# Seven block products for the second product of a feed-forward layer, in an fp32 kernel for one core

## The chip, the core and the metric

One NeuronCore of a Trainium2 chip runs the whole kernel. Its engines are TensorE (PE, matrix products; PEld is its weight load), VectorE (DVE), ScalarE (ACT), GpSimd (POOL) and SyncE (SP, which here only issues DMAs). Each engine works through its own list of instructions in order and waits at semaphores for the others. The metric is the device time of one execution, in microseconds (us).

## The reference, cut to what matters

```
x = attention(q, k, v)                       # retention, 4 x 576 tokens, 512 wide
h = x @ moe_w_in;  g = max(0.01*h, h);  y = g @ moe_w_out       # first layer
h = y @ moe2_w_in; g = h * cos(h);      out = g @ moe2_w_out    # second layer
```

There are 2304 tokens; both layers go from 512 to 2048 and back to 512, all in fp32. For accuracy the kernel splits each fp32 operand into a high part that TensorE takes exactly and the remainder, and adds three products (high by low, low by high, high by high). So each block product is made of three matmuls per 128 rows of depth.

## The kernel before, in words

**First part of the program.** Attention and the first layer run over five blocks of tokens (512, 512, 512, 384, 384), and the result y goes to DRAM. Beside this, the second layer's operands are prepared and stored in DRAM: `second_weights` (L1009) converts the weights of a pair of 128-wide slices of the hidden layer, `x_parts` (L902) makes the forms of y.

**Second layer, first product.** Tokens are taken in three blocks of 768 (two halves of 384), the hidden layer in eight pairs of slices. One block with one pair is a unit; there are 24 units. A unit is a 2 x 2 block product done with seven block products in place of eight (the scheme of Strassen and Winograd): sums and differences of the blocks of the weights (`wa`, `ws`) and of y (`xq`) are made beforehand, and partial results are shared between PSUM banks 4 to 7 by ScalarE copies (L1212). `i_mm` (L1106) is one such product: six matmuls of 128x128 by 128x384.

**Gate.** `gate` (L1130) makes g = h cos(h) of one 128x384 block at a time: copy or add out of PSUM, the integer number of turns (ScalarE), two steps that take the turns away (VectorE, L1150 and L1155), a sine and a square (ScalarE, L1162 and L1163), one product (VectorE, L1166), then the high part (ScalarE, L1173) and the remainder (VectorE, L1176).

**Second layer, second product.** `out_` (L1225) takes one token half, one of four output slices and one unit: two slices of the hidden layer, three matmuls each, six matmuls. Two units make a group that adds up in one PSUM bank (0 to 3); after each group VectorE adds the bank, times -2, to the sum in SBUF (L1258), or into the buffer that is stored. A group has 2 halves x 2 units x 4 slices = 16 such steps, and there are 12 groups.

**What sets the order.** `slots` is a list in program order: one second product behind about every first product, and what is left of each block at its end (`LATE`, `DRAIN`). Everything after the first block of tokens is then given as tasks to `Plan`, with an assumed duration, what it needs and a due time. `play` always takes, of the tasks that can begin first, the one that is due first, and so fixes the order of each engine's list, SP's too. Buffers are handed out in rings (`Ring`), and a ring's size decides when a load may start. `open_low` and `open_all` open the second layer's buffers when those of the first part are done with.

## Time and profile before

| | us |
|---|---|
| median of 3 runs | 855.56 (853.37 to 856.75) |
| the profiled execution | 853.42 |
| its span, first to last instruction | 851.3 |
| TensorE busy in the span | 829.3 (97%) |
| VectorE busy | 601.5 (71%) |
| ScalarE busy | 518.4 (61%) |

The span is the time between the first and the last instruction of the profiled execution; what lies around it is 2.1 us. Matrix instructions are pipelined, so the mean duration of one (334 ns) is longer than the distance between two; the distance is read from the chain of waits, which gives the length of a run of so many matmuls. The chain is followed back from the last instruction: at each step to whatever ended the wait, or to the instruction before on the same engine.

### The profile page before, as it was taken

How to read it: one execution, taken by the hardware profiler on the slowest of the kernel's cores; microseconds unless marked ns; L12 is line 12 of the kernel's file. 1: busy time of each engine (PE TensorE's matmuls, PEld its weight loads, DVE VectorE, ACT ScalarE, POOL GpSimd, SP SyncE). 2: the span in 40 equal slices, each digit the busy share in tenths (PEclk: the TensorE clock that was granted, in tenths of full speed). 3: DMA queues.
4: the chain of work that ended last, by engine and by line, in shares of the span. 5: the costliest groups of instructions: out<-in, count | busy, mean ns of one | idle time of the engine just before them, and what ended most of it. 6: DMA issues, size and time to landing. Idle time of an engine off the chain costs nothing.

```text
span 851.3 us, 16302 instructions
## 1 busy us (share of the span) xinstructions
PE 829.3 (97%) x6288; PEld 771.0 (91%) x6288; DVE 601.5 (71%) x1183; ACT 518.4 (61%) x1112; POOL 8.5 (1%) x9
## 2 busy tenths in 40 slices
PE   6699999999999999999999999999999999999998
PEld 6478888888888888999999999999999999999998
DVE  4799985776876757667511587889877876866762
ACT  4688864554655545555422688767678755677650
POOL 0000020000000000000000000000000000000000
PEclk7799999999999999999999999999999999999999
DMA  9925512656657866853790798798988697665312
GB/s 358 418 83 202 192 67 85 217 194 211 211 191 251 247 213 197 260 191 135 262 406 2 252 311 272 265 374 322 349 284 287 216 405 272 208 225 186 137 49 75
DMA packets 91949, 193.30 MB, mean 227 GB/s; under 512 B 7648, under 2 KB 55264, under 8 KB 81632
## 3 DMA queue, kind: packets, MB, share of 16 engines
q1 hardware_dynamic: 91728, 191.92, 64.2%
q8 instruction: 49, 0.80, 0.4%
q10 hardware_dynamic: 144, 0.35, 0.1%
q14 instruction: 28, 0.23, 0.1%
HBM read 143.22 MB, written 49.02 MB: 226 GB/s over the span
## 4 chain that ended last, share of the span: by engine, by line
PE 90%; DMA 4%; issue 3%; DVE 2%; ACT 1%; SPq 0%; POOLq 0%; DVEq 0%
PE psum L1239 23%; PE psum L519 22%; PE psum L505 21%; PE psum L1111 19%; DMA raw<-in_w 2%; PE psum L366 1%; PE psum L305 1%; PE psum L328 1%; PE psum L268 1%; DMA wa<-wa 1%; DMA ws<-ws 1%; DVE t L464 0%; DVE st L351 0%; DVE t L457 0%; DVE t L453 0%
## 5 line engine op out<-in xcount | busy, mean ns | idle before, releaser
L1239 PE MATMUL psum<-g,wo 128*128 128x384 f32 x1152 | 222.3, 334 | 0.0
L505 PE MATMUL psum<-x_sb,w 128*128 128x512 f32 (+1 forms) x960 | 214.2, 373 | 4.2 <-DVE x_sb L493 2.5
L519 PE MATMUL psum<-g,w 128*128 128x512 f32 (+1 forms) x960 | 212.0, 370 | 0.0
L505 PEld LDWEIGHTS psum<-x_sb,w 128*128 128x128 f32 x960 | 177.5, 190 | 29.7 <-DVE x_sb L493 2.7
L1239 PEld LDWEIGHTS psum<-g,wo 128*128 128x128 f32 x1152 | 201.7, 188 | 0.0
L519 PEld LDWEIGHTS psum<-g,w 128*128 128x128 f32 x960 | 174.3, 188 | 23.7
L1111 PE MATMUL psum<-x,ws 128*128 128x384 f32 x576 | 114.5, 335 | 1.3 <-ACT psum L1212 1.3
L1111 PEld LDWEIGHTS psum<-x,ws 128*128 128x128 f32 x576 | 100.9, 188 | 2.3 <-ACT psum L1212 1.9
L797 DVE TENSOR_TENSOR g<-graw,g 128x512 fp32r<-128x512 f32 (+1 forms) x64 | 39.9, 623 | 69.3 <-ACT g L794 69.0
L1111 PE MATMUL psum<-x,wa 128*128 128x384 f32 x432 | 86.1, 334 | 0.0
L1111 PEld LDWEIGHTS psum<-x,wa 128*128 128x128 f32 x432 | 75.9, 188 | 0.0
L1166 DVE SCALAR_TENSOR_TENSOR h<-r,h 128x384 f32<-128x384 f32 x96 | 52.9, 554 | 24.0 <-ACT r L1163 23.7
L794 ACT CAST g<-graw 128x512 fp32r<-128x512 f32 (+1 forms) x64 | 36.3, 568 | 48.8 <-PE psum L519 47.0
L790 ACT ACTIVATE graw<-psum 128x512 f32<-128x512 f32 (+1 forms) x64 | 34.7, 542 | 48.2 <-PE psum L505 47.5
L1162 ACT ACTIVATE r<-r 128x384 f32<-128x384 f32 x96 | 50.4, 525 | 21.2 <-DVE r L1155 20.7
L1150 DVE SCALAR_TENSOR_TENSOR r<-n,h 128x384 f32<-128x384 int32 x96 | 53.0, 552 | 11.9 <-ACT n L1147 11.5
L1176 DVE TENSOR_TENSOR g<-h,g 128x384 fp32r<-128x384 f32 x96 | 52.7, 553 | 10.9 <-ACT g L1173 10.3
L1147 ACT ACTIVATE n<-h 128x384 int32<-128x384 f32 x96 | 49.3, 519 | 8.4 <-DVE h L1139 8.0
L1155 DVE SCALAR_TENSOR_TENSOR r<-n,r 128x384 f32<-128x384 int32 x96 | 53.2, 554 | 1.6
L1173 ACT CAST g<-h 128x384 fp32r<-128x384 f32 x96 | 48.6, 509 | 7.6 <-DVE h L1166 7.3
L1163 ACT ACTIVATE r<-r 128x384 f32<-128x384 f32 x96 | 50.5, 526 | 2.0
L1258 DVE SCALAR_TENSOR_TENSOR acc<-psum,acc 128x384 f32<-128x384 f32 x48 | 26.7, 557 | 16.4 <-PE psum L1239 15.3
(81 smaller groups left out, 794.8 us busy)
## 6 DMA issues: line engine op xcount, KB each, us to landing
ws<-ws SPq DMA_DIRECT2D x24, 1024.0 KB, 7.1
wo<-wo SPq DMA_DIRECT2D x24, 1024.0 KB, 6.0
wa<-wa SPq DMA_DIRECT2D x24, 768.0 KB, 6.1
ch<-in_qkv SPq DMA_DIRECT2D x17, 1024.0 KB, 7.7
mraw<-in_w SPq DMA_DIRECT2D x64, 256.0 KB, 3.6
x<-xq SPq DMA_DIRECT2D x21, 768.0 KB, 9.6
raw<-in_w SPq DMA_DIRECT2D x15, 1024.0 KB, 9.1
xq<-m SPq DMA_DIRECT2D x84, 128.0 KB, 5.1
```

The costliest lines, as they stand in the source:

```text
L505: nc.tensor.matmul(hp, wt[:, i, cols], x_t[lj, k][:, j, :n], start=(k == 0 and a == 0), stop=(k == KK - 1 and a == 2),)
L519: nc.tensor.matmul(psum[:, BANK_O + m, :n], wt[:, i, cols], gt[:, j, :n], start=(f == 0 and a == 0), stop=(f == NF - 1 and a == 2),)
L1111: nc.tensor.matmul(bank[BANKS[m]], a[:, hl, i, j * P : (j + 1) * P], x[:, j, v, :], start=m in (1, 5) and j == 0 and n == 0, stop=j == 1 a ...
L1147: t = add("ACT", 515, lambda: nc.scalar.activation(n_ap(), hb.ap, AF.Copy, scale=INV_2PI), [t], due, 0, nb.old)
L1150: nc.vector.scalar_tensor_tensor(out=r_ap(), in0=n_ap(), scalar=-C1, in1=hb.ap, op0=ALU.mult, op1=ALU.add)
L1155: nc.vector.scalar_tensor_tensor(out=r_ap(), in0=n_ap(), scalar=-C2, in1=r_ap(), op0=ALU.mult, op1=ALU.add)
L1162: t = add("ACT", 515, lambda: nc.scalar.activation(r_ap(), r_ap(), AF.Sin, scale=0.5), [t], due)
L1163: t = add("ACT", 515, lambda: nc.scalar.activation(r_ap(), r_ap(), AF.Square), [t], due)
L1166: nc.vector.scalar_tensor_tensor(out=hb.ap, in0=r_ap(), scalar=0.5, in1=hb.ap, op0=ALU.subtract, op1=ALU.mult)
L1173: t = add("ACT", 515, lambda: nc.scalar.copy(gb.ap[:, 0], hb.ap), [t], due, 0, gb.old)
L1176: nc.vector.tensor_tensor(out=gb.ap[:, 1], in0=hb.ap, in1=gb.ap[:, 0].bitcast(F32), op=ALU.subtract)
L1239: nc.tensor.matmul(bank[m], wt[:, i, hl, m * P : (m + 1) * P], gt[:, v, :], start=h == 0 and z == 0 and x == 0, stop=h == 1 and z == 1 and ...
```

## The change

The first part of the program keeps its products. In the second layer:

- The second product is a 2 x 2 block product by seven products too. A group is again two units; its blocks are (hidden slice pair) by (token halves), and each product works on both units and one of two output slices `t`: 14 products of six matmuls per group. The order of the products is `OUT`; each `t` has two PSUM banks, `a` and `b`, and ScalarE copies `a` to `b` twice per group and `t` (`cp1`, `cp2`).
- Its weights are forms of w_out, `wp` (four) and `wq` (three) per pair of slices, made in `second_weights` with the factor -4 pi, in place of `wo`. Both rings hold two.
- The gate counts in turns: the forms of w_in carry the factor 1/(2 pi), so one step takes the turns away in place of two, and it works on two blocks (768 columns) at once. It also makes the sums that the seven products need (`tq`), and splits two blocks at a time.
- Weights are walked to and fro: the second block of tokens takes the pairs from the last to the first, so that the first two units of a block use the weights that lie there.
- TensorE's two kinds of products are two chains for the planner, no longer one. The forms of y for the second block of tokens are made in the first part of the program. The forms lie in DRAM and SBUF in pieces of 128 tokens, and a matmul of the first product reads its 384 columns as three pieces.

```diff
+OUT = (1, 6, 2, 7, 3, 5, 4)
+O_OF = {1: ("p", 0), 6: ("p", 1), 2: ("p", 2), 7: ("p", 3), 3: ("q", 0), 4: ("q", 1), 5: ("q", 2)}
-LATE, DRAIN = 12, 6
+LATE, LAST, DRAIN = 8, 10, 5
-N_G, N_WO, N_H = 16, 4, 6
+N_G, N_Z = 9, 2
...
-        todo = [x for g in range(n_unit // 2) for x in halves(g)]
+        todo = [("o", g, m, t) for g in range(n_unit // 2) for m in OUT for t in range(2)]
...
-                debt = min(debt + 8 / 7, 2.0) if ripe() else 0.0
+                debt = min(debt + 1, 2.0) if ripe() else 0.0
...
+            made, last = w_sums(*quarter, got, d[7], [(o2, 2), (o1, 3), (o1, 1), (o2, 0)], BACK)
+            last += [
+                parted(quarter[0], tb[0], [(o1, 0)], [made], d[7], BACK),
+                parted(lambda b=tb[1]: b.ap, tb[1], [(o1, 2), (o2, 1)], [made], d[7], BACK),
+            ]
...
+                if u >= NPAIR and u % NPAIR < 2:
+                    same = u - 1 - 2 * (u % NPAIR)
+                    w_buf[kind, u], w_task[kind, u] = w_buf[kind, same], w_task[kind, same]
...
-                        bank[BANKS[m]],
+                        bank[BANKS[m]].rearrange("p (q t) -> p q t", t=Q),
                         a[:, hl, i, j * P : (j + 1) * P],
-                        x[:, j, v, :],
+                        x[:, :, v, j, :],
...
-            t = dve(600, rest_a, [t], due, rb.old)
-            t = dve(560, rest_b, [t], due)
-            nb.users.append(t)
-            t = add("ACT", 515, lambda: nc.scalar.activation(r_ap(), r_ap(), AF.Sin, scale=0.5), [t], due)
-            t = add("ACT", 515, lambda: nc.scalar.activation(r_ap(), r_ap(), AF.Square), [t], due)
+            def turn():
                 nc.vector.scalar_tensor_tensor(
+                    out=rb.ap, in0=rb.ap.bitcast(I32), scalar=-1.0, in1=pair(), op0=ALU.mult, op1=ALU.add
+                )
+            t = dve(1040, turn, [t], due)
+            t = add("ACT", 885, lambda: nc.scalar.activation(rb.ap, rb.ap, AF.Sin, scale=PI), [t], due)
+            t = add("ACT", 885, lambda: nc.scalar.activation(rb.ap, rb.ap, AF.Square), [t], due)
...
+            t13 = dve(960, from_b, [*both, opened["all"]], due, tq.old)
+            t2 = dve(560, lambda: then(2, 2, 0), [t13], due)
+            two("z", z_ring, lambda: hb.ap[:, 3:4], 1, [t], hb)
+            t4 = dve(560, lambda: then(3, 3, 2), [t2], due)
+            two("u", g_ring, lambda: q(2, 4), 2, [t4], tq)
+            two("t", g_ring, lambda: q(0, 2), 2, [t13, t2], tq)
...
-            if h == 0:
+            if m == 1:
+                read_at[g, "cp1", t] = add(
+                    "ACT", 490, lambda: nc.scalar.copy(b, a), [got, b_free.get(t) or bank_free[2 + t][0]], due - SOON
+                )
                 return
...
+            if m == 2:
+                read_at[g, "cp2", t] = add(
+                    "ACT", 490, lambda: nc.scalar.copy(b, a), [read_at[g, 6, t], x], due - SOON
+                )
...
             (0, 0, at["H", 2, 4]), (0, 1, at["H", 2, 8]), (0, 2, at["H", 2, 12]),
+            (1, 0, at["H", 3, 4]), (1, 1, at["H", 3, 9]), (1, 2, at["H", 3, 14]),
```

How the lists move is shown at three places. First TensorE, where the first second products stand behind the third unit; before (L1111 is the first product, L1239 the second):

```order
L1111 MATMUL psum<-x_4506,wa_4510 128x384 x6
L1111 MATMUL psum<-x_4507,ws_4512 128x384 x6
L1239 MATMUL psum<-g_4876,wo_4514 128x384 x3
L1239 MATMUL psum<-g_4877,wo_4514 128x384 x3
L1111 MATMUL psum<-x_4508,ws_4512 128x384 x6
L1239 MATMUL psum<-g_4876,wo_4514 128x384 x3
L1239 MATMUL psum<-g_4877,wo_4514 128x384 x3
```

And now (L1143 is the first product, L1315 the second), four first products into the fourth unit:

```order
L1143 MATMUL psum<-x_4820,wa_4825 128x384 x6
L1315 MATMUL psum<-g_5109,wp_5104 128x384 x3
L1315 MATMUL psum<-g_5112,wp_5105 128x384 x3
L1315 MATMUL psum<-g_5109,wp_5104 128x384 x3
L1315 MATMUL psum<-g_5112,wp_5105 128x384 x3
L1143 MATMUL psum<-x_4821,ws_4827 128x384 x6
L1143 MATMUL psum<-x_4822,ws_4827 128x384 x6
L1143 MATMUL psum<-x_4823,wa_4825 128x384 x6
```

The first second product stood behind 19 first products and stands behind 25 now; a second product reads two units' weights (`wp_5104` and `wp_5105`) where it read one unit's.

Second, VectorE at the end of the program, where the last gate ends; before (L1176 is the remainder of g, L1258 the addition of a PSUM bank):

```order
L1166 SCALAR_TENSOR_TENSOR h_4864<-r_4871,h_4864 128x384
L1258 SCALAR_TENSOR_TENSOR acc_4891<-psum,acc_4891 128x384
L1176 TENSOR_TENSOR g_4890<-h_4864,g_4890 128x384
L1258 SCALAR_TENSOR_TENSOR acc_4891<-psum,acc_4891 128x384 x3
L1258 SCALAR_TENSOR_TENSOR out_4873<-psum,acc_4891 128x384
```

And now (L1352 adds a PSUM bank, L1232 and L1235 make the sums `tq`, L1214 is the remainder of a form):

```order
L1214 TENSOR_TENSOR z_5118<-h_4829,z_5118 128x384
L1352 TENSOR_TENSOR acc_5120<-psum,acc_5120 128x384
L1214 TENSOR_TENSOR z_5119<-h_5103,z_5119 128x384
L1214 TENSOR_TENSOR g_5114<-tq_5108,g_5114 128x2x384
L1232 TENSOR_TENSOR tq_5108<-h_5103 128x768
L1235 TENSOR_TENSOR tq_5108<-h_5103,tq_5108 128x384 x2
L1214 TENSOR_TENSOR g_5117<-tq_5108,g_5117 128x2x384
L1214 TENSOR_TENSOR g_5116<-tq_5108,g_5116 128x2x384
L1352 TENSOR_TENSOR acc_5120<-psum,acc_5120 128x384 x7
```

Behind the last gate's product stand a subtraction of two blocks, two more that hang on it, and three remainders, where one remainder stood; and the last addition of the group before the last (the first L1352 shown) now stands ahead of them.

Third, SP's list just ahead of the second layer's first loads; before (L880 stores a prepared form, L1091 loads weights, L1102 loads forms of y):

```order
L756 DMA y<-graw 128x384
L880 DMA wo_108<-mt 128x512
L880 DMA wo_108<-mraw 128x512
L880 DMA wo_108<-mt 128x512
L880 DMA wo_108<-mraw 128x512
L1091 DMA wa_4510<-wa_85 128x1536
L1091 DMA ws_4512<-ws_93 128x2048
```

And now (L886, L1123 and L1134 are the same three):

```order
L886 DMA xq_83<-mt 128x256 x3
L886 DMA xq_83<-more 128x256 x2
L886 DMA xq_83<-mt 128x256 x2
L886 DMA xq_83<-more 128x256 x6
L886 DMA xq_83<-mt 128x256
L886 DMA xq_83<-more 128x256
L1123 DMA wa_4824<-wa_85 128x1536
L1123 DMA ws_4826<-ws_93 128x2048
L1134 DMA x_4817<-xq_82 128x1536
```

The stores of the forms of y for the second block of tokens now stand ahead of the first load; before they stood among the second layer's loads.

## Rows read from the trace of the kernel before

**Rows 1.** The page, busy time of TensorE, its share of the span, instructions.
```profile
PE 829.3 (97%) x6288; PEld 771.0 (91%) x6288; DVE 601.5 (71%) x1183; ACT 518.4 (61%) x1112; POOL 8.5 (1%) x9
```

**Rows 2.** Span and mean granted TensorE clock of the core.
```profile
core 0: 851.3 us, clock 0.986
```

**Rows 3.** Stretches: length, PE, PEld, DVE, ACT, POOL busy, clock, DMA share, GB/s.
```profile
440.00:445.00 5.00, 5.00 (x31) 5.00 (x30) 0.56 (x1) 1.50 (x3) 0.00 (x0) 1.00 1.01 417
...
460.00:480.00 20.00, 20.00 (x117) 20.00 (x116) 5.59 (x11) 7.35 (x14) 0.00 (x0) 1.00 0.37 106
480.00:500.00 20.00, 18.75 (x106) 17.83 (x104) 15.62 (x31) 17.15 (x39) 0.00 (x0) 1.00 0.95 314
500.00:520.00 20.00, 19.92 (x115) 19.83 (x115) 16.36 (x34) 17.29 (x40) 0.00 (x0) 1.00 0.87 317
560.00:580.00 20.00, 20.00 (x117) 20.00 (x116) 16.46 (x33) 14.78 (x34) 0.00 (x0) 1.00 1.03 412
```

**Rows 4.** Groups of instructions by line, TensorE: shapes, count, busy us, mean ns, idle before.
```profile
L1239 PE MATMUL psum<-g,wo 128*128 128x384 f32 x1152 | 222.3, 334 | 0.0
...
L1111 PE MATMUL psum<-x,ws 128*128 128x384 f32 x576 | 114.5, 335 | 1.3 <-ACT psum L1212 1.3
...
L1111 PE MATMUL psum<-x,wa 128*128 128x384 f32 x432 | 86.1, 334 | 0.0
```

**Rows 5.** The chain that ended last, longest pieces: start us, us, what.
```profile
140.13 8.64 PE psum L505 x36
...
471.21 7.30 PE psum L1111 x42
...
487.34 6.70 DMA wa<-wa
...
819.75 28.10 PE psum L1239 x162
```

**Rows 6.** The chain's last piece.
```profile
847.87 0.56 DVE out L1258
```

**Rows 7.** Groups by line, VectorE.
```profile
L1155 DVE SCALAR_TENSOR_TENSOR r<-n,r 128x384 f32<-128x384 int32 x96 | 53.2, 554 | 1.6
...
L476 DVE TENSOR_TENSOR w<-t,w 128x1024 fp32r<-128x1024 f32 (+1 forms) x17 | 19.8, 1165 | 2.9 <-ACT w L473 2.9
...
L873 DVE TENSOR_TENSOR m<-m 128x512 fp32r<-128x512 f32 x24 | 16.3, 687 | 4.7 <-ACT m L869 4.0 <-DMA xq<-m 0.5
...
L890 DVE TENSOR_TENSOR m<-m 128x256 f32<-128x256 f32 x24 | 9.2, 420 | 1.4 <-DMA m<-y 1.3
```

**Rows 8.** Groups by line, ScalarE.
```profile
L1163 ACT ACTIVATE r<-r 128x384 f32<-128x384 f32 x96 | 50.5, 526 | 2.0
...
L1212 ACT COPY psum<-psum 128x384 f32<-128x384 f32 x48 | 22.4, 466 | 16.4 <-PE psum L1111 15.1
...
L446 ACT ACTIVATE raw<-raw 128x1024 int32<-128x1024 uint32 (+1 forms) x17 | 18.8, 1104 | 0.0
...
L473 ACT CAST w<-t 128x1024 fp32r<-128x1024 f32 (+1 forms) x17 | 17.1, 1004 | 2.8 <-DVE t L464 2.7
...
L869 ACT CAST m<-m 128x512 fp32r<-128x512 f32 x24 | 14.6, 617 | 5.1 <-DMA xq<-m 5.1
```

**Rows 9.** Instructions of VectorE in order of time: start us, us, what.
```profile
586.82 0.56 DVE L1139 TENSOR_TENSOR h<-psum,s 128x384 f32<-128x384 f32 x1
587.30 0.55 DVE L1166 SCALAR_TENSOR_TENSOR h<-r,h 128x384 f32<-128x384 f32 x1
```

**Rows 10.** DMA issues: line, count, KB each, median us from issue to landing.
```profile
ws<-ws SPq DMA_DIRECT2D x24, 1024.0 KB, 7.1
...
x<-xq SPq DMA_DIRECT2D x21, 768.0 KB, 9.6
```

**Rows 11.** SP's list in order of time: start us, us, what.
```profile
419.51 0.40 SPq L1091 DMA_DIRECT2D wa<-wa  x1
...
431.44 0.32 SPq L1091 DMA_DIRECT2D wo<-wo  x1
```

More of the change, by code (lines that the diff above doesn't have):

```diff
@@ L1150, in rest_a @@
+            half_done[u, m] = read
+            if m in (2, 3):
+                return read
+            first = m == 7
+            due = by["x" if first else "u"] - AHEAD
+            pair = lambda: hb.ap[:, 0:3:2] if first else hb.ap[:, 1:4:2]
+            rb = r_ring.next()
+            t = add(
+                "ACT", 885, lambda: nc.scalar.copy(rb.ap.bitcast(I32), pair()),
+                [read, half_done[u, 2 if first else 3]], due, 0, rb.old,
+            )
+            def turn():
                 nc.vector.scalar_tensor_tensor(
-                    out=r_ap(), in0=n_ap(), scalar=-C1, in1=hb.ap, op0=ALU.mult, op1=ALU.add
+                    out=rb.ap, in0=rb.ap.bitcast(I32), scalar=-1.0, in1=pair(), op0=ALU.mult, op1=ALU.add
@@ L1171, in gate @@
             rb.users.append(t)
[L1172 to L1182 removed]
+            half_done[u, first] = t
@@ new lines, in two, with lower @@
+            def two(kind, ring, src, n, needs, buf):
+                due = by[kind] - AHEAD / 4
+                gb = g_buf[u, kind] = ring.next()
+                def lower():
+                    nc.vector.tensor_tensor(
+                        out=gb.ap[:, :, 1], in0=src(), in1=gb.ap[:, :, 0].bitcast(F32), op=ALU.subtract
+                    )
+                h_ = add("ACT", 885 if n == 2 else 515, lambda: nc.scalar.copy(gb.ap[:, :, 0], src()),
+                         [*needs, opened["all"]], due, 0, gb.old)
+                t = dve(960 if n == 2 else 560, lower, [h_], due)
+                buf.users.append(t)
+                g_low_done[u, kind] = t
@@ new lines, in gate, with from_b, then @@
+            if first:
+                two("x", g_ring, pair, 2, [t], hb)
+                return read
+            tq = tq_ring.next()
+            both = [t, half_done[u, True]]
+            q = lambda i, j: tq.ap[:, i:j]
+            def from_b():
+                nc.vector.tensor_tensor(out=q(0, 2), in0=hb.ap[:, 1:3], in1=hb.ap[:, 0:2], op=ALU.subtract)
+            def then(i, b, a):
+                nc.vector.tensor_tensor(out=tq.ap[:, i], in0=hb.ap[:, b], in1=tq.ap[:, a], op=ALU.subtract)
@@ L1247, in out_ @@
[L1247 to L1259 removed]
+                            to,
@@ new lines, in mm @@
+                            wt[:, hl, i, t * P : (t + 1) * P],
+                            gt[:, fi, v, :],
+                            start=m in (1, 5) and h == 0 and x == 0,
+                            stop=h == 1 and x == 2,
+                            skip_group_check=True,
+                        )
+            got = last_pe["o"] = add("PE", 1042, mm, needs, due)
+            for u in us:
+                w_buf[kind, u].users.append(got)
+                g_buf[u, form].users.append(got)
@@ L1273, in out_ @@
-            bank_free[m] = [t]
+                x = add(
+                    "ACT", 490, lambda: nc.scalar.copy(kept(), to),
+                    [got, opened["all"], left.get((which, t))], due - SOON / 2,
+                )
+            else:
+                x = add("DVE", 560, lambda: nc.vector.tensor_tensor(out=kept(), in0=to, in1=kept(), op=ALU.add),
+                        [got], due - SOON / 2)
+            read_at[g, m, t] = x
+            if last and m in (2, 4):
+                leave(x, which, m == 4, 0)
@@ new lines, in out_, with more @@
+            if last and m == 5:
+                for w, half, other in ((1, 0, 3), (3, 1, 7)):
+                    def more(w=w):
+                        nc.vector.tensor_tensor(
+                            out=acc.ap[:, 2 * w + t], in0=acc.ap[:, 2 * w + t], in1=acc.ap[:, 8 + t], op=ALU.add
+                        )
+                    y = dve(560, more, [x, read_at[g, other, t]], due - SOON / 2)
+                    leave(y, w, half, 1)
+                    left[4, t] = y
+            if m == 2:
+                read_at[g, "cp2", t] = add(
+                    "ACT", 490, lambda: nc.scalar.copy(b, a), [read_at[g, 6, t], x], due - SOON
+                )
```

308 lines of the change are left out of this document (155 added, 153 removed).

## The prediction

> **What bounds the kernel now.** I read the page first. TensorE is busy for 97% of the span [rows 1] at a mean granted clock of 0.986 [rows 2], so the end is set by how much TensorE has to do, and the other engines matter only where they keep it waiting. The stretches show where that is. From 460 us on TensorE is busy for 20.00 us of 20 but for the beginning of the second layer, where 1.25 us are lost between 480 and 500 and 0.08 behind that, at a clock of 1.00 throughout [rows 3]. VectorE has some 16.4 us of work in 20 there. The chain agrees: its long pieces are TensorE's, it enters the second layer at 471.21 and leaves TensorE at 847.85, ahead of one last addition on VectorE [rows 5, 6]. Between these lie 376.6 us in which 1152 + 576 + 432 = 2160 matmuls of 384 columns run [rows 4].
>
> The price of one matmul is taken from the chain, not from its own duration: the last 162 take 28.10 us, 0.1735 us each; 42 at the stage's start take 7.30, the same [rows 5]. 2160 of them are 374.8 us, and with the 1.3 us of waits this is the stage to within half a microsecond. One block product (six matmuls) is 1.041 us.
>
> **What is removed.** A group has 14 products in place of 16, and there are 12 groups: 24 products or 144 matmuls fewer, 144 x 0.1735 = 25.0 us. All of them stand on the path, since TensorE has no gap in which they could hide. The page "TensorE: Matmul & The Clock Gate" of the Trainium skill (section Back-to-back issue gap) gives an isolated spacing of columns / 2.4 + 2.5 ns, which is 162.5 ns here, and for a stream of load and product 131 ns at 512 columns. By the first the gain would be 23.4 us, by the second under 19. The trace agrees with neither: 173.5 ns at 384 columns.
>
> **What is added on VectorE and ScalarE in the second layer.** VectorE's instructions take 420 ns at 256 columns, 687 at 512 and 1165 at 1024 [rows 7]; 768 lies half way between the last two, 0.93 us. Neighbours overlap: one of 0.56 us is followed 0.48 us later by the next [rows 9], so I count 0.48 for a narrow and 0.85 for a wide one. A unit now has two narrow additions out of PSUM, two wide steps that take the turns away, two wide products, one wide and two narrow sums, and three wide and one narrow remainder: 8 x 0.85 + 5 x 0.48 = 9.2 us. A group is two units and ten additions of a bank: 18.4 + 4.8 = 23.2 us in the 28 x 1.041 = 29.1 us that TensorE needs, 80%. Before it was 2 x 18 + 8 narrow ones, 21.1 in 31.2, 68%. In the first group of each token block the ten additions are copies on ScalarE. ScalarE: a copy out of PSUM is 466 ns, a wide cast lies between 617 and 1004, 0.81 us, a wide function between 526 and 1104, 0.87 [rows 8]; 8 x 0.47 + 5 x 0.81 + 4 x 0.87 = 11.3 us a unit of 14.6, 77%. So neither becomes the bound by its sum. What cover they lose is 12 points of VectorE's time, and it costs where a form that TensorE wants stands late in the list.
>
> To find such places I laid TensorE's new list out in steps of 1.041 us and asked of each form what VectorE must still do once the product it depends on has ended. Two places come out late.
>
> At the end of the first token block the second product of the third group (units 4 and 5) wants unit 5's sums 3.6 us after unit 7's sixth first product (three first products and half a second one stand between). VectorE's list has behind the addition that waits for that product a remainder, the sums (one wide, two narrow), a wide product and two remainders: 0.48 + 0.85 + 0.85 + 1.04 + 0.85 + 0.85 + 0.85 = 5.8 us. TensorE waits 2.2 us.
>
> At the end of the program no first product is left to fill in. After the last of these TensorE has 24 second products, 25.0 us. The last group's second product wants the last unit's sums after 10 + 2.5 products, 13.0 us. They are the last remainder on VectorE, and in the list they stand behind the addition for the tenth product, which cannot run before 10.4. From there: addition 0.48, two remainders 0.48 + 0.85, the wide sum 0.85, the first narrow sum 0.56, ScalarE's cast 0.81, one wide remainder 0.85 and the last 0.93: 16.2, with the hand-overs 16.3. TensorE waits 3.3 us. Loads do not add to it: the weights `wp` of that group can be issued 6.8 us ahead of their use, a load of 1 MB lands after 7.1 in the median [rows 10], and a delay there is swallowed by the same wait.
>
> **The copies inside PSUM.** Between the third product of a `t` and its fourth stand an addition on VectorE and a copy on ScalarE, 0.03 + 0.56 + 0.03 + 0.47 = 1.1 us with free engines (a hand-over takes 0.02 to 0.03 us, 847.85 to 847.87 at the end [rows 5, 6]). In TensorE's list one other product (1.04 us) covers it in the last two groups, two or three in the others. The nearest row is L1212: 48 such copies, for which TensorE waited 1.3 us in all [rows 4]. The bounds are 0 and, if each of the 24 found a wide instruction before it on both engines (0.85 + 0.87) behind two products, 24 x 0.75 = 18 us. I take 1.5, near the row.
>
> **Loads in the second layer.** Per unit 3.6 MB in place of 2.8, less the four units that reuse what lies there. The rings hold two, and both units' weights are read together, so `wp` for the next group starts only when the fourth product is done: 10 to 14 us ahead of its use in most groups by the same layout, against 7.1 landing. For x at a block's turn it is 8.3 us against a median of 9.6 under load [rows 10], with DMA at 412 GB/s at the turn before [rows 3]; I count 0 and keep 2 us a turn as the bound. The loads that cost 1.25 us at the stage's start have the same 7 to 9 us as before, so this wait stays.
>
> **The first part of the program.** TensorE's list there is the same instruction for instruction. VectorE gets some 29 us more (the sums and remainders of w_out, and the forms of y for the second token block, moved ahead), and over its idle time this costs nothing as long as it ends in time: the first loads of the second layer stand behind these stores on SP. Before, they were issued from 419.51 to 431.44 [rows 11] and DMA ran at 417 GB/s to 445 [rows 3]. VectorE's list has its last such instruction four steps later into the last token block (nine against five), 4 x 24 x 0.1735 = 16.7 us: first load at 436, and 2 x 1024 + 9 x 768 KB take 22 us at 417 GB/s, ready at 458 to 460 for a stage that begins at 471. If the cover of some 11 us is gone, each further microsecond costs one. The narrower stores of this part share DMA with little else, and I count nothing for them.
>
> **The sum.** Against the profiled execution of 853.42 us: -25.0 + 2.2 + 3.3 + 1.5 = -18.0, 835.4 us. The median of the runs shown is 855.56, 2.1 above the profiled one; taken from it, 837.5 us, which is the forecast.
>
> **Rivals.**
> *No new waits* (0.07). The layout counts each list as it stands, but VectorE may be ahead where I have it late: it idled 3.6 us of 20 in the stage before [rows 3]. Then only the 25.0 us are seen: 830.5. Against it stands the end, where nothing can fill in.
> *Forms late in every group* (0.12). In some ten places my layout leaves a form 1 to 2 us before it is wanted, without the cast of 0.81 us on ScalarE that lies between its sum and its remainder. If each costs 0.8 to 1.2 us, the gain shrinks by 8 to 12: 846 to 850. For it speaks that this cast shares ScalarE's list with eight other wide instructions a unit; against it that up to 25 first products run ahead of the second ones.
> *Slower: the bank copies decide* (0.03). If the addition and the copy stand behind wide instructions and a neighbour's product is no cover, each of the 24 pairs costs 0.03 + 0.85 + 0.56 + 0.03 + 0.87 + 0.47 - 1.04 = 1.8 us, 43 us in all: 880. It decides from 18.0 / 24 = 0.75 us per pair. The 1.3 us for 48 copies speak against it.
> *Slower: reading in three pieces* (0.02). The 1008 first products read 384 columns as three runs of 128. It decides from 18.0 us / 1008 = 18 ns per matmul; at 30 ns the time would be 868. Against it: 36 matmuls of 512 columns took 8.64 us, 0.469 ns a column [rows 5], and those of 384 take 0.452, so starting a run anew more often has cost nothing so far.
> *The change does not do what it says*: the list of TensorE has 1008 second-product matmuls, so this one falls.
>
> **Chances.** The forecast's case, 831.5 to 845, has 0.76; with the rivals above and its bounds (0 to 2 us a turn for x, 0 to 18 for the copies) the range is 830 to 848, leaving out the slow cases and half of the late forms. A difference of 0.5% (4.3 us) is about what a measurement of this kernel can tell from none. Faster by more than that (below 851.3): 0.76 + 0.07 + 0.10 = 0.93; within it 0.03; slower 0.04.
>
> **What would show it.** Right: 2016 matmuls of 384 columns in the second layer at 0.1735 us, TensorE's idle time there 6 to 10 us with the two longest gaps at the turn to the second token block and some 12 us before the end, each released by VectorE's remainder (L1214); the stage begins within 1 us of 471; VectorE near 80% in the stage. Wrong: waits of TensorE on loads of `wp` or x, on ScalarE's copies L1330 and L1369 beyond 3 us in all, another price per first-product matmul, or a stage that begins late.

## The result and the profile after

The changed kernel takes 842.65 us (median of 4 runs, 840.47 to 844.49), the kernel before on the same chip 855.84 (4 runs): ratio 0.985, 95% interval 0.982 to 0.988. It is 13 us faster, within the range forecast, and the gain is 5 us smaller than the forecast's.

The first row of the page after answers to [rows 1], the next to [rows 2]:

```profile
PE 808.8 (96%) x6144; PEld 747.2 (89%) x6144; DVE 645.1 (77%) x1141; ACT 542.9 (65%) x1038; POOL 8.6 (1%) x9
```
```profile
core 0: 838.3 us, clock 0.983
```

TensorE has 144 instructions fewer and 20.5 us less busy time, and its share has fallen by a point: it now waits. Where, the chain and the stretches tell. First the chain, at the first products of the second layer and near the end; 42 matmuls take 7.30 us as before [rows 5], but the 14 near the end take 0.28 us each:

```profile
472.18 7.30 PE psum L1143 x42
...
820.61 3.94 PE psum L1315 x14
```

The stage runs from 472.18 to the span's end, 366.1 us, where it was 471.21 to 851.3, 380.1 us: 14.0 less. Now TensorE's own part of it, before and after (length, then busy time and count of TensorE, its weight loads, VectorE, ScalarE and GpSimd, granted clock, DMA share, GB/s):

```profile
471.21:847.85 376.64, 375.29 (x2161) 373.96 (x2159) 279.34 (x552) 255.85 (x553) 0.00 (x0) 1.00 0.72 252
```
```profile
472.18:834.29 362.11, 354.37 (x2016) 349.90 (x2015) 296.43 (x438) 269.97 (x451) 0.00 (x0) 1.00 0.70 256
```

Read it as two sums. Idle time is length less busy: 1.35 us before, 7.74 after. And 2160 matmuls at 0.1735 us are 374.8, 2016 are 349.8: before, TensorE was busy for 0.5 us more than that, after for 4.6 more. So 25.0 us went, 6.4 came back as waits and 4.1 as matmuls that ran longer, and 14.5 are left (14.0 with what follows TensorE's last matmul). The profile models where a matmul ends, so the split of these 10.5 us is rough; their sum is not.

The waits by what ended them (total us, times, longest):

```profile
PE psum L1315 <- ACT g L1218: 2.4, 1, 2.4
PE psum L1143 <- DMA ws<-ws: 1.5, 1, 1.5
PE psum L1315 <- DVE g L1214: 1.2, 2, 0.7
PE psum L1143 <- DMA x<-xq: 1.1, 2, 0.6
PE psum L1143 <- ACT psum L1276: 1.0, 2, 0.5
PE psum L1315 <- ACT psum L1369: 0.3, 1, 0.3
```

Only the L1276 line was there before, with 1.3 us [rows 4, there L1212]. It is one wait, and not the price of 48 copies: in ScalarE's list an instruction of 1.28 us, ACT_TABLE_LOAD, stands ahead of the stage's first sine, and the copy that TensorE wants stands behind both. Before:

```profile
479.03 1.28 ACT L1162 ACT_TABLE_LOAD   x1
481.84 1.31 PE L1111 MATMUL psum<-x,ws 128*128 128x384 f32 x6 [1.25 <-ACT psum L1212]
```

It is there in the changed kernel too, and TensorE waits 0.53 us behind it:

```profile
481.25 1.28 ACT L1197 ACT_TABLE_LOAD   x1
484.19 2.38 PE L1143 MATMUL psum<-x,ws 128*128 128x384 f32 x12 [0.53 <-ACT psum L1276]
```

The others, in TensorE's list in order of time, with the idle time ahead in brackets: a load of weights early on, the turn from the first block of tokens to the second, and the end.

```profile
507.68 2.36 PE L1143 MATMUL psum<-x,ws 128*128 128x384 f32 x12 [1.48 <-DMA ws<-ws]
565.83 1.28 PE L1143 MATMUL psum<-x,wa 128*128 128x384 f32 x6 [0.64 <-DMA x<-xq]
567.63 1.31 PE L1143 MATMUL psum<-x,ws 128*128 128x384 f32 x6 [0.51 <-DMA x<-xq]
570.33 1.66 PE L1315 MATMUL psum<-g,wp 128*128 128x384 f32 x8 [0.70 <-DVE g L1214]
...
819.62 0.53 PE L1315 MATMUL psum<-g,wp 128*128 128x384 f32 x1 [2.42 <-ACT g L1218]
820.61 2.86 PE L1315 MATMUL psum<-g,wp 128*128 128x384 f32 x8 [0.46 <-DVE g L1214]
```

At the end TensorE does one matmul between 817.20 and 820.61, and what follows is slow. In stretches of 2 us (same columns as above) the granted clock falls to 0.50 right behind the gap, the lower of TensorE's two levels, and is at 1.00 again from 824:

```profile
818.00:820.00 2.00, 0.38 (x1) 0.19 (x1) 1.94 (x4) 1.56 (x3) 0.00 (x0) 0.96 0.75 300
820.00:822.00 2.00, 1.54 (x5) 1.39 (x5) 0.56 (x1) 0.00 (x0) 0.00 (x0) 0.50 0.00 0
822.00:824.00 2.00, 2.00 (x9) 2.00 (x9) 0.00 (x0) 0.00 (x0) 0.00 (x0) 0.69 0.00 0
824.00:826.00 2.00, 1.90 (x11) 1.58 (x11) 0.94 (x2) 0.46 (x1) 0.00 (x0) 1.00 0.00 1
```

VectorE is busy all through that gap. Its list there, up to what TensorE waits for:

```profile
810.56 0.95 DVE L1201 SCALAR_TENSOR_TENSOR h<-r,h 128x768 f32<-128x768 f32 x1
...
815.57 0.95 DVE L1214 TENSOR_TENSOR g<-tq,g 128x768 fp32r<-128x768 f32 x1
816.55 0.96 DVE L1232 TENSOR_TENSOR tq<-h 128x768 f32<-128x768 f32 x1
817.55 1.15 DVE L1235 TENSOR_TENSOR tq<-h,tq 128x384 f32<-128x384 f32 x2
818.62 1.94 DVE L1214 TENSOR_TENSOR g<-tq,g 128x768 fp32r<-128x768 f32 x2
```

The last unit's h is complete at 811.5 us (L1201), but its sums (L1232) begin only at 816.55: the sums have one buffer, and the unit before still reads it at 815.57.

The wait for weights at 507.68 has its cause on SyncE. Its list there:

```profile
496.19 4.86 SPq L886 DMA_DIRECT2D xq<-m  x8
501.14 0.39 SPq L1123 DMA_DIRECT2D ws<-ws  x1
```

Eight stores of the third block's x forms are issued from 496.19 on, some of them after a wait for the remainder they store, and the load stands behind them. It is issued at 501.14, 29.0 us after the stage's begin, and used at 507.68. The run e9_two_late below makes these forms later: there the load is issued 24.0 us after the begin and TensorE does not wait for `ws`. In e1_two_tq the load stands behind the same eight stores, at 29.0 us, and does not cost a wait, because four second products stand ahead of its use. So both the place of the load and TensorE's order count.

### The profile page after: what moved, and what is told of

The parts are those of the page before. It is cut to its first block, busy times and chain, and to the rows that moved or that the text cites. A ratio compares the mean times of both kernels' runs of the same rounds, so it can differ in the third digit from the quotient of the medians.

```text
span 838.3 us, 16086 instructions
## 1 busy us (share of the span) xinstructions
PE 808.8 (96%) x6144; PEld 747.2 (89%) x6144; DVE 645.1 (77%) x1141; ACT 542.9 (65%) x1038; POOL 8.6 (1%) x9
## 4 chain that ended last, share of the span: by engine, by line
PE 84%; DVE 5%; DMA 5%; issue 3%; ACT 2%; SPq 0%; DVEq 0%; POOLq 0%; ACTq 0%
PE psum L524 22%; PE psum L510 20%; PE psum L1315 19%; PE psum L1143 18%; DMA raw<-in_w 2%; PE psum L371 1%; PE psum L333 1%; PE psum L310 1%; DMA ws<-ws 1%; PE psum L273 1%; DVE g L1214 1%; DVE acc L1352 1%; DMA mraw<-in_w 1%; DMA xq<-m 1%; DVE t L462 0%
## 5 line engine op out<-in xcount | busy, mean ns | idle before, releaser
L1143 PE MATMUL psum<-x,ws 128*128 128x384 f32 x576 | 112.1, 335 | 3.0 <-DMA ws<-ws 1.5
L1143 PEld LDWEIGHTS psum<-x,ws 128*128 128x128 f32 x576 | 100.7, 188 | 4.3 <-DMA ws<-ws 1.8
L1315 PE MATMUL psum<-g,wp 128*128 128x384 f32 x432 | 84.6, 340 | 4.0 <-ACT g L1218 2.4
L1143 PE MATMUL psum<-x,wa 128*128 128x384 f32 x432 | 85.4, 335 | 0.6 <-DMA x<-xq 0.6
L1315 PE MATMUL psum<-g,wq 128*128 128x384 f32 x432 | 82.3, 334 | 0.1
L1315 PEld LDWEIGHTS psum<-g,wp 128*128 128x128 f32 x432 | 76.3, 190 | 6.0 <-ACT g L1218 2.7
L1143 PEld LDWEIGHTS psum<-x,wa 128*128 128x128 f32 x432 | 75.7, 188 | 1.1 <-ACT r L1198 0.9
L1315 PEld LDWEIGHTS psum<-g,wq 128*128 128x128 f32 x432 | 75.5, 188 | 0.4 <-DVE acc L1352 0.4
L1352 DVE TENSOR_TENSOR acc<-psum,acc 128x384 f32<-128x384 f32 x90 | 49.6, 554 | 16.7 <-PE psum L1315 16.5
L1201 DVE SCALAR_TENSOR_TENSOR h<-r,h 128x768 f32<-128x768 f32 x48 | 45.7, 952 | 15.2 <-ACT r L1198 15.1
L1214 DVE TENSOR_TENSOR g<-tq,g 128x768 fp32r<-128x768 f32 x48 | 45.6, 953 | 6.8 <-ACT g L1218 6.2
L1192 DVE SCALAR_TENSOR_TENSOR r<-r,h 128x768 f32<-128x768 int32 x48 | 45.5, 952 | 1.8 <-ACT r L1187 1.6
L1197 ACT ACTIVATE r<-r 128x768 f32<-128x768 f32 x48 | 40.7, 847 | 8.7 <-DVE r L1192 8.6
L1187 ACT CAST r<-h 128x768 int32<-128x768 f32 x48 | 40.1, 836 | 8.2 <-DVE h L1173 7.9
L1218 ACT CAST g<-tq 128x768 fp32r<-128x768 f32 x48 | 40.1, 837 | 6.0 <-DVE tq L1235 4.2
```

The source lines that it names most:

```text
L1143: nc.tensor.matmul(bank[BANKS[m]].rearrange("p (q t) -> p q t", t=Q), a[:, hl, i, j * P : (j + 1) * P], x[:, :, v, j, :], start=m in (1, 5 ...
L1187: "ACT", 885, lambda: nc.scalar.copy(rb.ap.bitcast(I32), pair()),
L1192: nc.vector.scalar_tensor_tensor(out=rb.ap, in0=rb.ap.bitcast(I32), scalar=-1.0, in1=pair(), op0=ALU.mult, op1=ALU.add)
L1197: t = add("ACT", 885, lambda: nc.scalar.activation(rb.ap, rb.ap, AF.Sin, scale=PI), [t], due)
L1201: nc.vector.scalar_tensor_tensor(out=pair(), in0=rb.ap, scalar=0.5, in1=pair(), op0=ALU.subtract, op1=ALU.mult)
L1214: nc.vector.tensor_tensor(out=gb.ap[:, :, 1], in0=src(), in1=gb.ap[:, :, 0].bitcast(F32), op=ALU.subtract)
```

## The experiments

Because a planner orders every engine's list, an edit moves more than its own instructions. And the first part of the program is not equally long in every run: in the profiled runs below the second layer begins between 472.2 and 476.8 us, with a granted clock of 0.57 to 0.75 in the stretch from 20 to 40 us, which does not go with it. So beside the median of the times I give the stage: from the first product of the second layer in the chain (begin) to the end of the span. Each stage is that of one profiled run; how much it varies from run to run is not shown.

| run | time us | begin | span | stage | TensorE idle | matmuls longer by |
|---|---|---|---|---|---|---|
| before | 855.84 | 471.21 | 851.3 | 380.1 | 1.4 | 0.5 |
| after | 842.65 | 472.18 | 838.3 | 366.1 | 7.7 | 4.6 |
| e1_two_tq | 839.40 | 474.43 | 836.5 | 362.1 | 5.4 | 2.9 |
| e2_whole_x | 845.32 (one run) | 476.81 | 843.2 | 366.4 | 7.6 | 4.9 |
| e3_no_walk | 847.21 | 474.42 | 843.4 | 369.0 | 9.7 | 5.5 |
| e4_x_late | 854.38 | 474.91 | 852.3 | 377.4 | 12.6 | 10.9 |
| e5_twice | 860.39 | 476.06 | 859.2 | 383.1 | 2.0 | 1.9 |
| e6_pool_q | 848.04 | 474.75 | 846.7 | 372.0 | 10.9 | 7.1 |
| e4_pool_q | 872.52 | 472.65 | 873.3 | 400.7 | 29.0 | 17.1 |
| e8_again | 851.16 | 474.51 | 849.7 | 375.2 | 12.9 | 8.0 |
| e9_two_late | 842.05 | 472.26 | 837.5 | 365.2 | 6.6 | 4.8 |
| e7_warm | 842.74 | 474.89 | 839.7 | 364.8 | 4.7 | 3.2 |
| b2_z_first | 838.00 | 475.26 | 836.4 | 361.1 | 4.3 | 3.1 |
| b3_z_two | 835.77 | 473.35 | 832.7 | 359.4 | 3.5 | 2.1 |

(Idle: from the begin to TensorE's last matmul, less its busy time there. Longer: busy time less 0.1735 us for each matmul.)

Where I say that a kernel loses time at a place, it is read from the starts of TensorE's matmuls in the trace: what the distance from one to the next has above 0.1735 us, added up. The changed kernel loses 1.8 us at the load of `ws`, 2.7 at the turn and 6.2 from 805 us on, 5.1 of these at the last gap and right behind it.

**What a product is worth.** The first second product of a group is done twice:

```
-            got = last_pe["o"] = add("PE", 1042, mm, needs, due)
+            if m == 1:
+                got = last_pe["o"] = add("PE", 2084, lambda: (mm(), mm()), needs, due)
+            else:
+                got = last_pe["o"] = add("PE", 1042, mm, needs, due)
```

> The first of the seven second products (m = 1) is computed twice per group and output row block: the second time starts the sum afresh, so the result is the same. It adds 24 products of six matmuls, 144 in all, as many as the change took away. Theory: TensorE sets the pace of this stage and a product costs what its matmuls cost, 144 x 0.1735 = 25.0 us, less about 2 to 3 us in the last group, where TensorE stands idle for 3.4 us behind exactly this product and then runs at a lower granted clock. Stage 388 to 391 us against 366.1, time 864.5 to 867.5. Rival: in a good part of the groups TensorE waits in effect for VectorE and ScalarE, and the added products fill those waits: stage under 384, time under 860.

Measured: 860.39 us (859.52 to 861.32), stage 383.1, 17.0 more than without. The theory's 22 to 25 fell; the stage is the rival's, the time 0.4 us above its bound. But the reason is not a cheaper product. TensorE runs 144 matmuls more at the same price, and nearly all waits of the stage are gone with them, not those of the last group alone. All that is left:

```profile
PE psum L1143 <- ACT psum L1276: 1.0, 2, 0.5
PE psum L1315 <- ACT g L1218: 0.5, 1, 0.5
PE psum L1315 <- ACT psum L1372: 0.3, 1, 0.3
```

Idle time falls by 5.7 and the excess of the matmuls by 2.7: 25.0 - 8.4 = 16.6, and 17.0 with the tail. So the product's price is right, and most of the changed kernel's waits come of TensorE's thinner list. In that the rival was nearer than the theory.

**The end: one buffer for the sums.** A second buffer (and, for room, eight buffers of forms and not nine):

```
-        g_ring, z_ring, tq_ring, r_ring = Ring(N_G), Ring(N_Z), Ring(1), Ring(2)
+        g_ring, z_ring, tq_ring, r_ring = Ring(N_G), Ring(N_Z), Ring(2), Ring(2)
-N_G, N_Z = 9, 2
+N_G, N_Z = 8, 2
```

> The changed kernel with two buffers for the gate's sums (tq) in place of one, and eight buffers for g in place of nine to make room. Theory (the end waits because the last unit's sums stand behind the release of the one tq buffer): the wait of some 3.9 us in the last 25 us shrinks to about 1, the clock does not fall there (it lost some 1.5 us in the changed kernel), and the time is 3 to 5 us below the changed kernel's 842.65, about 838.5. Rival (the end is set by the gate's own chain through ScalarE, or eight buffers for g cost as much elsewhere): the wait stays within 1 us of what it was or returns at another place, 841 to 844.

Measured: 839.40 us (838.76 to 840.89), ratio to before 0.9825 (0.9808 to 0.9843); stage -4.0. The three largest waits, and the stretch behind the last gap with its clock:

```profile
PE psum L1315 <- DVE g L1214: 1.5, 1, 1.5
PE psum L1143 <- DVE h L1173: 1.1, 1, 1.1
PE psum L1143 <- DMA wa<-wa: 1.0, 1, 1.0
```
```profile
818.00:820.00 2.00, 2.00 (x11) 2.00 (x12) 2.00 (x4) 0.78 (x2) 0.00 (x0) 1.00 1.03 427
```

The end's wait is halved, the one at the turn and the one for `ws` are gone, and two smaller ones have come. The clock stays at 1.00 behind the shorter gap. Of the 4.0 us, 2.6 are gained from 805 us on, where the theory had them; the turn and `ws` give 4.1 and new waits take 2.7, which the theory did not name.

**The clock behind the gap.** 18 matmuls that do no work fill the gap (into the bank `BANKS[5]`, behind the last group's first product):

```
+            if (g, m, t) == (n_unit // 2 - 1, 6, 0):
+                last_pe["o"] = add("PE", 3120, warm, [last_pe["o"], done[us[1], "s5"]], due)
```

> In the last group 18 idle matmuls (3.1 us) are put into a free bank right behind the first second product, where TensorE stood idle for about 3.4 us waiting for the last unit's sums. They do no work. Theory: TensorE stays busy through the gap, so the granted clock stays at 1.00 between 818 and 824 us, the 14 matmuls behind it take 0.17 to 0.19 us each and not 0.28, and the kernel gains 1.5 us: stage 364.6, time 841.1. Rival: the clock falls there for another reason: 14 matmuls again at about 0.28 us, stage 366, time 842.6; or the idle matmuls delay the sums, 843 and more.

Measured: the clock stays at 1.00 through the gap's place; stage -1.3, near the 1.5 expected, and all of it at the end. The median, 842.74 us (841.20 to 844.69), shows no difference, so the gain rests on the profiled runs alone; in this one the first part is 2.7 us longer.

```profile
820.00:822.00 2.00, 2.00 (x14) 2.00 (x13) 1.93 (x4) 1.84 (x3) 0.00 (x0) 1.00 1.03 420
```

So the fall of the clock is the gap's doing. In the changed kernel the 32 matmuls from 820.61 to the last weights (`wq`, 827.88) take 7.27 us, 1.7 more than at 0.1735; here 36 take 7.00, 0.75 more. The clock is worth about 1 us. The Trainium skill ("TensorE: Matmul & The Clock Gate", section HAM oscillation) says that waits between groups of matmuls can throttle TensorE again and that the price is paid behind each; in the changed kernel the trace agrees at this one gap of the stage. Behind gaps of the same kind the clock also falls in e2_whole_x and e8_again (0.50) and e9_two_late (0.54).

**The order of the products.** Product 2 needs only z, product 6 the longest chain of sums (u). In this kernel 2 goes first, and the copy ahead of the fourth product stands behind 6:

```
-OUT = (1, 6, 2, 7, 3, 5, 4)
+OUT = (1, 2, 6, 7, 3, 5, 4)
```

> One edit in the changed kernel: the second products go in the order 1, 2, 6, 7, 3, 5, 4 instead of 1, 6, 2, 7, 3, 5, 4, and the copy before the fourth stands behind product 6. Product 2 needs one form only (z, from h's last part), product 6 needs the longest chain of sums (u). Theory: u is due 2.08 us later in every group, so in the last group TensorE computes product 2 while VectorE finishes u: of the 3.4 us idle there and the lower clock behind it 2 to 3.5 us go, and the 0.70 us wait at the turn too: stage 362 to 364, time 838.5 to 840.5. Rival: the last unit's sums end where they ended, and product 6 waits as long behind product 2, or z comes late: stage 365.5 to 368.

Measured: 838.00 us (837.29 to 838.81), ratio 0.9802 (0.9783 to 0.9821); stage -5.0, more than the 2 to 4 expected. No wait on `ws` or x is left in its trace, and the end's gap is one of 1.65 us on the copy of product 1. From 805 us on 3.3 us less are lost and at the turn 1.5 less, as the theory has it; that the 1.8 us on `ws` are gone it did not foresee, nor the 1.6 us lost anew between 690 and 693 us.

> The order of b2_z_first and the second buffer for the sums of e1_two_tq (with 8 buffers of forms). Theory: the two take away parts of the same wait, the last group's, and with both nothing of it is left: stage 360 to 361, time 837 to 838.5, below e1_two_tq (stage 362.1, time 839.4). Rival: the waits return elsewhere (weights, block turn), since both only shift when the forms are made: stage 362 or more, time 839 or more.

Measured, with both edits: 835.77 us (834.90 to 836.58), ratio to before 0.9776 (0.9757 to 0.9794); stage 359.4, under the 360 to 361 expected. This is the best version, faster than both kernels: its ratio to before lies under the changed kernel's 0.9818 to 0.9881, 6.9 us between the medians. What is left of waits in its stage:

```profile
PE psum L1315 <- DVE g L1214: 2.0, 2, 1.1
PE psum L1143 <- ACT psum L1276: 1.0, 2, 0.5
```

A third one is 0.4 us, on a copy of product 1. The theory's reason fell: the last group's waits are not gone, 3.9 us are lost from 805 us on where b2_z_first loses 2.9. What is gone is every loss between the first 20 us of the stage and there.

**x in three pieces.** One piece of 384 columns in DRAM, SBUF and at the matmul:

```
-            some(pool, "x", [P, NQ, 2, 2, Q], F32R, x_buf.values())
+            some(pool, "x", [P, 2, 2, W], F32R, x_buf.values())
-                        x[:, :, v, j, :],
+                        x[:, j, v, :],
```

> The changed kernel with the forms of y stored and read in one piece of 384 columns, as before the change. Theory (reading three runs of 128 costs nothing): a run of first products takes 0.1735 us a matmul as in the changed kernel, 42 of them 7.30 us, and the profiled time stays within 3 us of 840.5; the stores of the forms are of 512 byte pieces again, which the first part hides. Rival (the pieces cost): first products become faster per matmul by up to 5 ns, 1008 x 5 ns = 5 us.

Measured once: 845.32 us, but the first part was 4.6 us longer; 42 matmuls take 7.30 us here too, and the stage is 366.4 against 366.1. At the matmul the pieces cost nothing that this run shows.

**The walk of the weights.** Each block takes the pairs in the same order and loads all of them:

```
-            return u % NPAIR if u // NPAIR % 2 == 0 else NPAIR - 1 - u % NPAIR
+            return u % NPAIR
-                if u >= NPAIR and u % NPAIR < 2:
+                if False:
```

> The changed kernel with the weights taken in the same order in every token block, so that the first two units of a block load theirs again: 14 MB more to load, at the turns of the token blocks, where the forms of y are loaded too. Theory (loads at the turn are just in time: TensorE waited 1.1 us for x there): waits on loads at the two turns grow by 3 to 8 us in all, 846 to 851. Rival (DMA has room, 0.74 to 0.93 of its time busy there): under 1.5 us, 841 to 844.

Measured: 847.21 us (845.62 to 851.47), ratio 0.9922 (0.9891 to 0.9953); stage +2.9, in the fastest of the four runs. The time is in the theory's range, but not for its reason: TensorE waits for `wp` only 0.4 us. What has grown is the turn, 2.31 us on ScalarE's cast (L1218) and 1.30 on the remainder, with a clock of 0.91 from 560 to 580 us. The walk is worth some 3 us of stage, but not mainly as a load that comes in time; how the missing loads help the turn I have not settled.

**Where the x forms are made.** The change moved the making of the second block's forms of x from the second layer into the first. Back to the second layer with it:

```
-            (1, 0, at["H", 3, 4]), (1, 1, at["H", 3, 9]), (1, 2, at["H", 3, 14]),
-            d = at["i", 2 + 4 * q, 1]
-            when(d, lambda q=q, d=d: x_parts(2, q, d, False))
+            for n, u in ((1, 1 + 2 * q), (2, 8 + 3 * q)):
+                d = at["i", u, 1]
+                when(d, lambda n=n, q=q, d=d: x_parts(n, q, d, False))
```

> The changed kernel with the forms of y for the second and third token block made in the second layer at the places of the kernel before: some 11 us of VectorE's work leave the first part and join the second layer's first block. Theory (TensorE is the bound, VectorE's sum of work does not matter but its place in the list does): the second layer starts up to 1 us earlier, TensorE's waits change by under 4 us, 841 to 846. Rival (VectorE at 80% and more paces the second layer): the time grows by 8 us or more, 850 and above.

Measured: 854.38 us (847.96 to 857.61, 10 runs), ratio 0.9985 (0.996 to 1.0009); stage +11.3. My theory fell: with the forms of both blocks made at these places the time is that of the kernel before. The waits were on x read back late (3.9 us) and on `ws` (1.7), but also on ScalarE and VectorE, and one of them shows a chain through a buffer. ScalarE's cast waits until a store has emptied its buffer, a copy out of PSUM stands behind it, and TensorE waits for that copy:

```profile
526.31 0.62 ACT L872 CAST m<-m 128x512 fp32r<-128x512 f32 x1 [1.55 <-DMA xq<-m]
...
528.17 0.47 ACT L1348 COPY acc<-psum 128x384 f32<-128x384 f32 x1
```
```profile
528.70 1.34 PE L1315 MATMUL psum<-g,wq 128*128 128x384 f32 x6 [1.33 <-ACT acc L1348]
```

So I next believed that the stores and SyncE's list were the price, and moved the second layer's stores to GpSimd's queue, in both kernels:

```
-                        nc.sync.dma_start(d, s_)
+                        (nc.gpsimd if own else nc.sync).dma_start(d, s_)
```

> The stores of the third token block's x forms (made in the second layer) are issued by GpSimd's queue and not by SyncE's, on which the weights are loaded. Theory: the load of unit 4's weights stood on SyncE behind eight stores that waited for VectorE, and the 1.5 us for which TensorE waited on it go: stage 364.6, time 841.1. Rival: the wait only covered another (on the sums, on x), and the time stays within 0.7 us of 842.6.

> As e4_x_late (the x forms of token blocks 1 and 2 made in the second layer again, stage 377.4 us), but their stores are issued by GpSimd's queue, so that no load of SyncE stands behind a store that waits for VectorE. Theory: what cost 11.3 us in e4_x_late is mostly the queue, weights and x that come late behind stores: stage 370 or less, time 847 or less. Rival: it is the work itself, VectorE and ScalarE being late with the forms of the groups in which x is made: stage 375 or more, time 852 or more.

Measured: 848.04 us (846.78 to 849.15), stage +5.9, and 872.52 us (871.13 to 875.46), stage +23.3 over e4_x_late. In the first both expectations fell; in the second the theory fell, and the loss is far beyond what the rival would explain. In the first the load of `ws` was issued 24.1 us after the begin and its wait was gone, but one store landed late and ScalarE's cast waited for it, this time for 5.49 us. Between the cast and the matmuls in the chain of e6_pool_q lie a remainder and an addition on VectorE:

```profile
500.81 8.74 DMA xq<-m
...
509.62 0.63 ACT m L872
...
511.48 11.13 PE psum L1143 x54
```

This showed the hold of a buffer that a store must empty, not the price of SyncE's list. Why that store took so long is open: the DMA engines were busy all the time from 505 to 510 us (share 1.01), and in the median these stores landed after 4.2 us, against 4.9 from SyncE in the changed kernel. The Trainium skill ("Trainium Kernel Development and Optimization", section Key Constraints) says that issuing DMAs from several engines only saves issue time. The trace agrees that SyncE's list gets shorter; each store takes GpSimd 547 ns instead.

The next kernel has e4_x_late's work in the second layer without its stores: the second block's forms are made early and used, and made once more late, for nothing.

```
-                parts_done.setdefault(n, []).extend(last)
+            if kept:
+                parts_done.setdefault(n, []).extend(last)
+            for n, u, kept in ((1, 1 + 2 * q, False), (2, 8 + 3 * q, True)):
```

> The changed kernel with the work of e4_x_late in the second layer, but without its stores: block 1's x forms are made in the first layer and stored, as in the changed kernel, and are made once more in the second layer (same loads, same 12 sums, 12 casts and 12 remainders) with nothing stored and nothing that waits for them; block 2's are made at e4_x_late's places. Theory: in e4_x_late the price was in what stands behind the stores (SyncE's queue, buffers that a store must empty before ScalarE may cast the next piece, x that is read back late), not in VectorE's and ScalarE's time: stage within 3 us of 366.1, time 841 to 846. Rival: the engines' time itself delays the forms of the groups: stage 374 or more, time 850 or more, as e4_x_late.

Measured: 851.16 us (849.99 to 853.33), stage +9.1. The rival was right. Two things were edited at once, so the other, the later place of the third block's forms, was run alone:

```
-            d = at["i", 2 + 4 * q, 1]
+            d = at["i", 8 + 3 * q, 1]
```

> The changed kernel with one edit: the making of block 2's x forms begins at units 8, 11 and 14 of the second layer, where e4_x_late and e8_again have it, and not at units 2, 6 and 10. No work is added. It tells apart the two edits in e8_again (stage 375.2 us). Theory: the added work of block 1 on VectorE and ScalarE costs most of e8_again's 9.1 us, and the place of block 2 little: stage 365 to 369, time 842 to 846. Rival: the place of block 2, nearer to its use and to the last units, costs most of it: stage 372 or more, time 848 or more.

Measured: 842.05 us (839.65 to 842.66), stage -0.9, as the theory has it. So the added work, with the order that the planner makes of it, costs 10.0 us of stage: 12 remainders of 684 ns, 12 sums of 419 ns and 12 casts of 624 ns, 13.2 us on VectorE and 7.5 on ScalarE, for results that nobody waits for.

Some of it is seen where the added work stands. Between 505 and 545 us e8_again loses 3.6 us and e9_two_late nothing. VectorE works through its list, the last two of the added remainders (L881) are in it, and the addition that TensorE's next product needs (here L1174) stands behind them:

```profile
535.65 0.68 DVE L881 TENSOR_TENSOR m<-m 128x512 fp32r<-128x512 f32 x1
536.50 0.69 DVE L881 TENSOR_TENSOR m<-m 128x512 fp32r<-128x512 f32 x1 [0.16 <-ACT m L872]
537.43 0.56 DVE L1215 TENSOR_TENSOR z<-h,z 128x384 fp32r<-128x384 f32 x1 [0.24 <-ACT z L1219]
537.91 1.01 DVE L1174 TENSOR_TENSOR h<-psum,s 128x384 f32<-128x384 f32 x2
```
```profile
538.51 2.35 PE L1144 MATMUL psum<-x,wa 128*128 128x384 f32 x12 [2.04 <-DVE h L1174]
```

The larger part, 6.4 us more than in e9_two_late, is lost between 630 and 700 us, about 100 us and more behind the last added instruction. What the traces show there is that the third block's forms, the work that does have a use, come later: the last of their remainders begins 143 us after the stage's begin in the changed kernel, 191 in e9_two_late, 202 in e8_again and 207 in e4_x_late, and at the turn to the third block (675 to 700 us) these lose 0, 2.0, 6.3 and 4.7 us. That the one is the cause of the other was not tested.

So the work can cost about what e4_x_late lost without any store of it. That it is what cost the 11.3 us there is not shown: e4_x_late loses 7.8 us at its waits on x, where e8_again waits for x 0.2 us in all. Open is also which share of the 10.0 us is VectorE's and which ScalarE's, and how much of it is the planner's new order.

## Why the prediction was right, and where it was not

*What is removed* was right: 2016 matmuls, 7.30 us for 42, and e5_twice puts them back at that price.

*VectorE and ScalarE* came out near the forecast as shares: 296.43 of 362.11 us is 82% (80 forecast), 269.97 is 75% (77). But VectorE's twelve groups of 23.2 us are 278; they leave out the third block's forms of y, some 13 of the 296. The estimated durations were low for wide remainders and products (0.95 against 0.93) and casts (0.84 against 0.81), high for the functions (0.85 against 0.87). "Neither becomes the bound by its sum" holds, but the sums were nearer to an edge than I said: e8_again adds 13.2 us to VectorE's 296 and 7.5 to ScalarE's 270 and loses 10.

*The turn* (2.2 forecast): 0.70 us on VectorE's remainder, and 1.15 on x, which I counted at 0 with a bound of 2. *The end* (3.3 forecast): 2.42 + 0.46 = 2.9. The place and the engine were right, and e1_two_tq shows the cause that my layout had implied without naming it: the sums' only buffer. *The copies in PSUM* (1.5 forecast): 0.3 on the fourth product's. The row taken as nearest, 1.3 us on L1212, and the 1.25 us that the paragraph on loads puts down to loads at the stage's start are the same wait, the one behind ACT_TABLE_LOAD. *Loads* had one miss, the 1.5 us on `ws`. I looked at when a buffer comes free and not at what stands ahead of the load in SyncE's list.

*The first part*: no first load is waited for, as forecast. The stage begins 0.97 us later, within the microsecond given; by the other runs that can be chance.

The step that failed is *the sum*. It counts each wait at its own length. The idle time came out almost as forecast, 6.4 us more than before against 7.0, but that is luck: the 1.5 us on `ws` and 1.15 on x, both put at nothing, stand in for what the turn, the end and the copies fell short of. And 4.1 us came on top, in matmuls that ran longer than 0.1735 us: -25.0 + 6.4 + 4.1 = -14.5, where I had -18.0. The clock at the end is about 1 to 1.5 of it. The rest lies around the nine gaps, some 0.3 us each: matmuls overlap, so that in the list 12 take 2.24 us where 12 x 0.1735 is 2.08, and ahead of a gap that overlap is lost; and six behind a gap take 1.28 or 1.31 us where they take 1.20 without. By the starts of the matmuls the end's gap cost 5.1 us, for which I had 3.3. In the table the excess goes with the idle time in every changed kernel, 0.5 to 1.0 of it. Of the 5 us that the forecast misses, these are 3.5; the later begin of the stage is one more, and what follows TensorE's last matmul is half a microsecond longer.

Of the rivals, *no new waits* and *bank copies* fell by the rows above, *three pieces* by e2_whole_x. *Forms late in every group* (846 to 850) did not happen; e8_again takes 851.16 us, but by waits at some places, not in every group. The prediction gave the move of the x forms no value at all; in e4_x_late, without it and with the third block's forms later, 11.3 of the 14.0 us of stage are lost.

Of the signs that the prediction names, the idle time (7.74 us), VectorE's share and the price of a matmul are there. But the second longest gap is the one on `ws`, and one of its signs of being wrong came too: TensorE waits on loads of x, 1.15 us at the turn.

## What to carry to other kernels

When TensorE is the bound and loses work, the other engines' lists get tighter even where their sums have room; look at what stands in a list ahead of the one instruction that TensorE needs, and move work that has no due date out of the stage (11.3 us of stage in e4_x_late). Count each wait of TensorE at its idle time in the trace and some 0.3 us more, and add what the granted clock loses behind it. Of two products that may change places, let the one with the shorter chain of inputs go first: here that gave 5.0 us of stage, 3.3 of them at the end.

## What was not expected of the hardware

The granted clock fell to 0.50 behind the changed kernel's last gap, and stayed at 1.00 behind the shorter one of e1_two_tq. One ACT_TABLE_LOAD of 1.28 us ahead of the stage's first sine reaches TensorE, 1.25 us before and 0.53 after. Stores issued by GpSimd took that engine 547 ns each in e6_pool_q, and one landed 8.74 us after its issue, with the DMA engines full, while ScalarE waited for it. And the beginning of the program is not equally fast in every run: in kernels with the same list of TensorE up to the second layer, the same 36 matmuls of the first part begin between 140.13 and 142.82 us. The granted clock in the stretch from 20 to 40 us, between 0.57 and 0.75, does not explain it: with 0.71 (before) and 0.63 (after) they begin at the same 140.13.
